# A recurrence and an ELU MLP on one core: the lead-in written in a fixed order, weights fetched in half-step parts on two queues

## The chip, the core and the metric

One core of a Trainium2 chip runs the whole kernel. The metric is device time in microseconds (us) of one launch, the lower the better; the median of three runs of the kernel before is 706.36 us (705.92 to 708.71). Five engines work side by side, each through its own list of instructions in order: PE (matmuls), DVE (vector), ACT (activation functions and copies), POOL (a second, slower elementwise engine) and SP, which here issues transfers and moves nothing else. A transfer (DMA) is issued by an engine's queue and lands later; whoever needs the data waits for it to land.

## What is computed

A gated linear recurrence per head, then an MLP with the ELU function, cut to what matters:

```python
f = 1.0 / (1.0 + np.exp(-f_logit))                 # (B, H, S, D) = (4, 8, 768, 48)
for t in range(S):
    state = f[:, :, t, :, None] * state + np.einsum('bhd,bhe->bhde', k[:, :, t], v[:, :, t])
    y[:, :, t] = np.einsum('bhd,bhde->bhe', q[:, :, t], state)
x = y.transpose(0, 2, 1, 3).reshape(B * S, H * D)  # 3072 x 384
h = x @ w_in                                       # 384 x 2048
g = np.where(h > 0.0, h, np.exp(np.minimum(h, 0.0)) - 1.0)
out = g @ w_out                                    # 2048 x 384
```

The weights arrive as 64-bit floats, 8 bytes an element, 12.6 MB in all.

## The kernel before

**Units.** The 3072 tokens are cut into 12 units of 256 tokens (`U`, `NU`), each of two chunks of 128 (`C`, `NCU`); three units make one batch entry, and the state runs through these three. Heads lie in pairs (`HP` is 4): heads 2p and 2p+1 on the two halves of the partitions, 256 token columns a pair.

**The gates of a unit** (`prepare`, L484). ACT takes Exp of the negated logits (L491), POOL adds 1 (L492), DVE multiplies up along the tokens of one chunk with a scan (L496) and takes the reciprocal (L499). q is multiplied with the reciprocal on DVE (L502), k with the running product on POOL (L503). `fine` (L505) only watches for overflow.

**The recurrence of a unit** (`attention`, L586). For each chunk: `transposed` (k turned on PE, L513, copied by ACT, L515), `scores` (k by q on PE, L524, masked on DVE, L529), `advance` (the state's step: PE L542, DVE L549 and L552), `outputs` (PE L565 and L573, copied to the tile `xt` by ACT, L577). After the second chunk six small transfers inside the core (L584, "the relocations") move the last heads' rows of `xt` to where the MLP wants them.

**The MLP of a unit** has 16 steps, one per 128 columns of the hidden width. `up` (L602): three matmuls into `psH` (two buffers), ACT's Relu and Exp (L611, L612), and DVE's combination of both into `gg` (L614). `down` (L618) follows two steps later (`HLAG`): matmuls of `gg` with `wo` into `psM`.

**The weights** are fetched and turned to 32-bit floats once, while unit 0 runs. `fetch(n)` (L433) brings what step n needs, 128 columns of `w_in` in four transfers and 128 rows of `w_out` in one, 0.786 MB in all, into one of three buffers `raw`. `convert(n)` (L448) does it in integer arithmetic: ACT rounds the low words (L462) and squares the high ones (L463), DVE builds the new bits in two instructions (L464, L468), POOL adds the rounding (L471), and DVE writes `wi` and `wo` (L479), with tiny values set to zero.

**The order** is written in `fast` from L644 on, and a scheduler then places each instruction on its engine: it may pull later work ahead where it thinks that an engine is free. In the first unit's loop (L661 to L682, m = 0) each step converts the weights of one step ahead of its `up`. From unit 1 on nothing is converted.

Of the kernel before, what the change touches and what calls it, by code (L numbers as in the profile page):

```python
# [355 lines left out]
def fast(ctx: ExitStack, tc: tile.TileContext, q, k, v, f_logit, w_in, w_out, out, flag):  # L356
# [23 lines left out]
    HLAG = 2  # L380
    LIMIT = 2.0**60
# [13 lines left out]
    def load(u):  # L395
        b, s0 = u // UPB, (u % UPB) * U
        for n in "fkq":
            for r in range(2):
                nc.sync.dma_start(
                    out=qkf[u % NB][n][HALF[r]],  # L400
                    in_=src[n][b, r::2, :, s0 : s0 + U].rearrange("p d s -> d p s"),
                )
# [3 lines left out]
    for i in range(NB):  # L406
        for n, to in (("f", 50.0), ("k", 0.0), ("q", 0.0)):
            (nc.gpsimd if i else nc.vector).memset(qkf[i][n][:], to)
        if i == 0:
            load(0)  # L410
# [9 lines left out]
    )  # L420
    fine = cst.tile([128, HP, NCU], FP32, name="fine")
# [10 lines left out]

    def fetch(n):  # L433

        c = slice(n * 128, (n + 1) * 128)
        if wide:
            raws[n] = sb.tile([128, 2 * DM], w_in.dtype, tag="raw", name=f"raw{n}", bufs=3)
            di, do = raws[n][:, 0:DM].rearrange("p (k f) -> p k f", k=NKT), raws[n][:, DM:]
        else:
            di, do = wi[:, :, c], wo[:, n, :]  # L440
        main = w_in[0 : NKT * 2 * D, c].rearrange("(k r d) f -> r d k f", r=2, d=D)
        rest = w_in[NKT * 2 * D :, c].rearrange("(k r d) f -> r d k f", r=2, d=PAD)
        for r in range(2):
            nc.sync.dma_start(out=di[64 * r : 64 * r + D], in_=main[r])
            nc.sync.dma_start(out=di[64 * r + D : 64 * r + 64], in_=rest[r])
        nc.sync.dma_start(out=do, in_=w_out[c, :])

    def convert(n):  # L448
# [22 lines left out]
        nc.gpsimd.tensor_tensor(out=bits[:], in0=bits[:], in1=rnd[:], op=ALU.add)  # L471
        val = bits[:].bitcast(FP32)

        for o, a, b in (
            (wi[:, :, n * 128 : (n + 1) * 128], sq[:, 0:DM], val[:, 0:DM]),
            (wo[:, n, :].unsqueeze(1), sq[:, DM:], val[:, DM:]),
        ):
            m = o.shape[1]
            nc.vector.scalar_tensor_tensor(  # L479
                out=o, in0=a.rearrange("p (k f) -> p k f", k=m), scalar=(1.125 * 2.0**-15) ** 2,  # L480
                in1=b.rearrange("p (k f) -> p k f", k=m), op0=ALU.is_ge, op1=ALU.mult,
            )

    def prepare(u):  # L484

        t = qkf[u % NB]
        g = gts[u] = sb.tile([128, HP, U], FP32, tag="g", name=f"g{u}")
        p_ = pts[u] = sb.tile([128, HP, U], FP32, tag="p", name=f"p{u}")
        for h in range(2):
            s = slice(2 * h, 2 * h + 2)  # L490
            nc.scalar.activation(g[:, s], t["f"][:, s], AF.Exp, scale=-1.0)  # L491
            nc.gpsimd.tensor_scalar_add(g[:, s], g[:, s], 1.0)  # L492
            for p in (2 * h, 2 * h + 1):
                for c in range(NCU):
                    a = g[:, p, c * C : (c + 1) * C]
                    nc.vector.tensor_tensor_scan(  # L496
                        out=a, data0=a, data1=a, initial=1.0, op0=ALU.mult, op1=ALU.max
                    )
                    nc.vector.reciprocal(p_[:, p, c * C : (c + 1) * C], a)  # L499
                    if c < NCU - 1:  # L500
                        yield
                nc.vector.tensor_tensor(out=t["q"][:, p], in0=t["q"][:, p], in1=p_[:, p], op=ALU.mult)  # L502
                nc.gpsimd.tensor_tensor(out=t["k"][:, p], in0=t["k"][:, p], in1=g[:, p], op=ALU.mult)  # L503
                yield
        nc.vector.scalar_tensor_tensor(  # L505
            out=fine[:], in0=g[:, :, C - 1 :: C], scalar=LIMIT, in1=fine[:], op0=ALU.is_le, op1=ALU.mult
        )

    def transposed(u, c):

        pt = ps.tile([128, HP, 128], FP32, tag="t", name=f"psT{u}_{c}")
# [43 lines left out]
    def outputs(u, c):  # L555
# [13 lines left out]
        if not first:  # L569
            s = sts.pop((u, c))  # L570
# [158 lines left out]
```

## Time and profile before

| what | value |
|---|---|
| median of 3 runs | 706.36 us |
| the profiled execution: its time / its span | 707.93 us / 706.1 us |
| PE busy in the span | 634.7 us (90%) |
| DVE, ACT, POOL busy | 300.8, 229.3, 105.5 us |
| granted TensorE clock, mean | 0.977 of full speed |
| moved by DMA | 38.04 MB, mean 54 GB/s |

The profiled execution took 707.93 us, 1.6 us over the median of the three runs and 1.8 us over its own span (706.1 us, first to last instruction). A row of a timeline gives the start in us, the duration, the engine, the line of the kernel, the operation, what it writes and reads, how many instructions are merged, and in brackets how long the engine stood idle just before and what released it. PE busy is the share of time in which a matmul was under way, not its speed. PEld is the load of a matmul's stationary side, beside PE.

### The profile page before, as it was taken

Reading aid. Unit: us, or ns where it says so; the run is one execution under the profiler, and the core shown is the slowest. Engines: PE = TensorE matmul, PEld = TensorE weight load, DVE = VectorE, ACT = ScalarE, POOL = GpSimd, SP = SyncE. Lnnn points to the kernel's source line nnn. Section 1 sums busy time; section 2 is a strip of 40 time slices with the busy share of each in tenths; the row PEclk is TensorE's granted clock in tenths of the full one; section 3 lists DMA queues with packets and bytes.
Section 4 is the critical chain, followed back from the end, with each engine's and each line's share of the span. In section 5 each row is a group of like instructions: output and inputs, shape, how many; then the busy total and the mean of one; then the engine's idle time right before and its main releaser. Section 6 shows DMA issues by size and latency. Waiting matters only on the chain.

```text
span 706.1 us, 9060 instructions
## 1 busy us (share of the span) xinstructions
PE 634.7 (90%) x3410; PEld 452.4 (64%) x3410; DVE 300.8 (43%) x599; ACT 229.3 (32%) x509; POOL 105.5 (15%) x102
## 2 busy tenths in 40 slices
PE   0768844569999999999999999999999999999996
PEld 0546522337677777777777777777777777777774
DVE  5889543438852722737124435471226221211110
ACT  2322342343433332333333432423333322333322
POOL 6333223223521101103001101110000000000000
PEclk9999898789999999999999999999999999999999
DMA  9564343432911200200101102011000000000000
GB/s 200 113 124 106 102 123 117 125 77 66 208 24 45 73 23 23 73 23 23 51 23 45 29 27 57 15 45 50 1 24 7 22 1 7 24 1 6 23 0 28
DMA packets 33525, 38.04 MB, mean 54 GB/s; under 512 B 4160, under 2 KB 31424, under 8 KB 33472
## 3 DMA queue, kind: packets, MB, share of 16 engines
q1 hardware_dynamic: 33472, 37.37, 21.2%
q8 instruction: 29, 0.48, 0.3%
q14 instruction: 24, 0.20, 0.1%
HBM read 31.46 MB, written 4.72 MB: 51 GB/s over the span
## 4 chain that ended last, share of the span: by engine, by line
PE 72%; DVE 0%; ACT 0%; issue 0%
PE psH L606 32%; PE psM L624 30%; PE psS L524 3%; PE psY L565 3%; PE psY L573 2%; PE psU L542 1%; PE psT L513 1%; DVE g L496 0%; ACT o L631 0%; DVE gg L614 0%; PE psF L641 0%
## 5 line engine op out<-in xcount | busy, mean ns | idle before, releaser
L606 PE MATMUL psH<-xt,wi 128*128 128x256 f32 x1152 | 295.9, 394 | 23.1 <-DVE wi L479 22.5
L624 PE MATMUL psM<-wo,gg 128*128 128x384 f32 x768 | 283.7, 493 | 13.9 <-DVE gg L614 13.8
L606 PEld LDWEIGHTS psH<-xt,wi 128*128 128x128 f32 x1152 | 216.1, 194 | 89.7 <-DVE wi L479 30.7
L614 DVE SCALAR_TENSOR_TENSOR gg<-e,psH 128x256 f32<-128x256 f32 x192 | 79.6, 414 | 320.6 <-ACT e L612 320.5
L624 PEld LDWEIGHTS psM<-wo,gg 128*128 128x128 f32 x768 | 146.3, 192 | 81.5 <-DVE gg L614 19.9
L611 ACT ACTIVATE e<-psH 128x256 f32<-128x256 f32 x192 | 73.8, 384 | 356.8 <-PE psH L606 353.5
L499 DVE RECIPROCAL p<-g 128x128 f32<-128x128 f32 x96 | 85.2, 920 | 0.3
L612 ACT ACTIVATE e<-e 128x256 f32<-128x256 f32 x192 | 80.0, 417 | 6.0
L503 POOL TENSOR_TENSOR k<-k,g 128x256 f32<-128x256 f32 x48 | 35.0, 746 | 225.4 <-DMA k<-in_k_dram 188.7
L496 DVE TENSOR_TENSOR_SCAN g<-g 128x128 f32<-128x128 f32 x96 | 39.4, 459 | 17.1 <-POOL g L492 17.1
L492 POOL TENSOR_SCALAR g<-g 128x512 f32<-128x512 f32 x24 | 35.4, 1491 | 67.7 <-ACT g L491 67.7
L471 POOL TENSOR_TENSOR bits<-bits,rnd 128x768 int32<-128x768 int32 x16 | 28.9, 1809 | 78.0 <-DVE bits L468 67.0
L524 PEld LDWEIGHTS psS<-q,k 48*128 48x128 f32 x384 | 29.2, 206 | 17.5 <-issue 11.3
L524 PE MATMUL psS<-q,k 48*128 48x128 f32 x384 | 36.5, 313 | 4.0 <-DVE q L502 2.6
L529 DVE TENSOR_TENSOR at<-psS,causal 128x512 f32<-128x512 f32 x48 | 30.9, 681 | 19.8 <-PE psS L524 19.8
L513 PE MATMUL psT<-ident,k 128*128 128x128 f32 x80 | 15.3, 301 | 22.3 <-POOL k L503 22.3
L577 ACT COPY xt<-psY 128x512 f32<-128x512 f32 x24 | 14.0, 585 | 51.1 <-PE psY L573 41.5
L565 PEld LDWEIGHTS psY<-at,v 128*48 128x48 f32 x384 | 21.6, 129 | 13.2 <-issue 6.5
L513 PEld LDWEIGHTS psT<-ident,k 128*128 128x128 f32 x80 | 10.7, 149 | 29.7 <-POOL k L503 24.4
L565 PE MATMUL psY<-at,v 128*48 128x128 f32 x384 | 28.8, 291 | 0.7 <-ACT xt L577 0.7
L515 ACT COPY kn<-psT 128x512 f32<-128x512 f32 x20 | 11.7, 586 | 39.9 <-PE psT L513 39.9
L573 PE MATMUL psY<-q,state 48*48 48x128 f32 x320 | 22.4, 281 | 0.0
(37 smaller groups left out, 188.4 us busy)
## 6 DMA issues: line engine op xcount, KB each, us to landing
raw<-in_moe_w_out_dram SPq DMA_DIRECT2D x16, 384.0 KB, 3.8
v<-in_v_dram SPq DMA_DIRECT2D x12, 384.0 KB, 4.0
raw<-in_moe_w_in_dram SPq DMA_DIRECT2D x32, 144.0 KB, 2.9
f<-in_f_logit_dram SPq DMA_DIRECT2D x24, 192.0 KB, 4.7
k<-in_k_dram SPq DMA_DIRECT2D x24, 192.0 KB, 4.0
q<-in_q_dram SPq DMA_DIRECT2D x24, 192.0 KB, 4.8
out_dram<-o SPq DMA_DIRECT2D x24, 192.0 KB, 1.9
raw<-in_moe_w_in_dram SPq DMA_DIRECT2D x32, 48.0 KB, 2.8
```

The lines of the kernel that those rows point to most:

```text
L492: nc.gpsimd.tensor_scalar_add(g[:, s], g[:, s], 1.0)
L496: nc.vector.tensor_tensor_scan(out=a, data0=a, data1=a, initial=1.0, op0=ALU.mult, op1=ALU.max)
L499: nc.vector.reciprocal(p_[:, p, c * C : (c + 1) * C], a)
L503: nc.gpsimd.tensor_tensor(out=t["k"][:, p], in0=t["k"][:, p], in1=g[:, p], op=ALU.mult)
L524: nc.tensor.matmul(pc[r][:, p], lhsT=t["k"][HALF[r], p, cols], rhs=t["q"][HALF[r], p, cols], start=True, stop=True,)
L565: nc.tensor.matmul(py[HALF[r], p, :], lhsT=vts[u][:, c, h * D : (h + 1) * D], rhs=at[:, r, p], start=(p == 0), stop=first, skip_group_chec ...
L573: nc.tensor.matmul(py[HALF[r], p, :], lhsT=s[HALF[r], p], rhs=t["q"][HALF[r], p, cols], start=False, stop=True, skip_group_check=True,)
L606: nc.tensor.matmul(ph[:], lhsT=wi[:, kt, s * 128 : (s + 1) * 128], rhs=xts[m][:, kt, :], start=(kt == 0), stop=(kt == NKT - 1),)
L611: nc.scalar.activation(e[:], ph[:], AF.Relu, scale=-1.0)
L612: nc.scalar.activation(e[:], e[:], AF.Exp, scale=-1.0)
L614: nc.vector.scalar_tensor_tensor(out=gs[T][:], in0=e[:], scalar=-1.0, in1=ph[:], op0=ALU.add, op1=ALU.max)
L624: nc.tensor.matmul(pms[m][i][:], lhsT=g[:, i * 128 : (i + 1) * 128], rhs=wo[:, s, :], start=(s == 0), stop=(s == NFT - 1),)
```

## The change

In code the change does the following.

- The stretch up to the end of unit 0's MLP stands under `manual_schedule`: its instructions keep the order in which they are written. Work of later units may still be placed between them.
- The two halves of unit 0's f, k and q and of each part of `w_in` go out on two queues, SP's and ACT's (`v`, `w_out` and the later units on SP's alone). Unit 0's logits are the first transfer on both; before, unit 0's `v` (0.39 MB) and a piece of `w_in` (0.15 MB) stood ahead of them on SP. The memsets of unit 0's tiles are shared by DVE and POOL.
- `fetch(n)` brings a part instead of a step: 256 columns of `w_in`, or 256 rows of `w_out`, each 0.786 MB and enough for two steps. Seven buffers `raw` instead of three (`AHEAD`); the order is in `parts`.
- `convert(n)` no longer writes `wi` and `wo`; `place(n)` does, in one instruction of 768 columns instead of two of 384. The rounded words are written back into `raw`, every second 32-bit word, and POOL reads them there. In step s of unit 0 stand `convert(s + 2)`, `place(s + 1)`, `up(s)`, a fetch, `down(s - 2)`.
- The gates: ACT adds the 1 itself (a Copy with a bias). Unit 0 is handled chunk by chunk, two pairs at a time; for all other units one scan runs over 256 columns, made to start again at the second chunk by a tile `restart` and a zero in `f`.
- The recurrence of the next unit stands four steps later in the MLP of a unit (`todo.get(s - 4, ())`); gates are made one unit ahead instead of two.

The core of the diff:

```diff
     def fetch(n):
-        c = slice(n * 128, (n + 1) * 128)
+        j, out_ = parts[n]
+        c = slice(j * 256, (j + 1) * 256)
+        to = wo[:, 2 * j : 2 * j + 2] if out_ else wi[:, :, c]
...
+        for r, e in enumerate((nc.sync, nc.scalar)):
+            e.dma_start(out=to[64 * r : 64 * r + D], in_=main[r])
+            e.dma_start(out=to[64 * r + D : 64 * r + 64], in_=rest[r])
...
-        nc.gpsimd.tensor_tensor(out=bits[:], in0=bits[:], in1=rnd[:], op=ALU.add)
+        nc.gpsimd.tensor_tensor(out=bits[:], in0=bits[:], in1=rnd, op=ALU.add)
+        nc.scalar.activation(sq[:], raw.bitcast(FP32)[:, 1::2], AF.Square)
+        vals[n] = sq, bits
+    def place(n):
...
+        nc.vector.scalar_tensor_tensor(
+            out=to, in0=sq[:].rearrange("p (k f) -> p k f", k=m), scalar=(1.125 * 2.0**-15) ** 2,
+            in1=bits[:].bitcast(FP32).rearrange("p (k f) -> p k f", k=m), op0=ALU.is_ge, op1=ALU.mult,
+        )
...
+            nc.scalar.activation(a, a, AF.Exp, scale=-1.0)
+            nc.scalar.activation(a, a, AF.Copy, bias=1.0)
...
         for s in range(NFT):
             T = m * NFT + s
-            for f in todo.get(s, ()):
+            for f in todo.get(s - 4, ()):
                 f()
-            if m == 0 and ready < NFT:
-                if ready + 1 < NFT:
-                    fetch(ready + 1)
-                convert(ready)
-                ready += 1
+            if m == 0:
+                if s + 2 < NFT:
+                    convert(s + 2)
+                if s + 1 < NFT:
+                    place(s + 1)
             up(T)
+            if m == 0 and s + AHEAD < NFT:
+                fetch(s + AHEAD)
```

DVE in the middle of unit 0's MLP, before: one step's conversion between two `gg` (`gg_4` is step 4's).

```order
L614 SCALAR_TENSOR_TENSOR gg_4_504<-e_4_501,psH_4_497 128x256
L464 TENSOR_SCALAR bits_449<-raw_396 128x768
L468 SCALAR_TENSOR_TENSOR bits_449<-raw_396,bits_449 128x768
L479 SCALAR_TENSOR_TENSOR wi<-sq_448,bits_449 128x3x128
L479 SCALAR_TENSOR_TENSOR wo<-sq_448,bits_449 128x384
L614 SCALAR_TENSOR_TENSOR gg_5_540<-e_5_537,psH_5_533 128x256
```

The same place now, with two masks of unit 1's recurrence in it.

```order
L653 SCALAR_TENSOR_TENSOR gg_3_396<-e_3_393,psH_3_389 128x256
L479 TENSOR_SCALAR bits_410<-raw_241 128x768
L483 SCALAR_TENSOR_TENSOR bits_410<-raw_241,bits_410 128x768
L499 SCALAR_TENSOR_TENSOR wi<-sq_381,bits_382 128x3x256
L653 SCALAR_TENSOR_TENSOR gg_4_424<-e_4_421,psH_4_417 128x256
L568 TENSOR_TENSOR at_0_433<-psS_0_0_434,causal 128x512
L568 TENSOR_TENSOR at_0_433<-psS_0_1_435,causal 128x512
L479 TENSOR_SCALAR bits_447<-raw_322 128x768
```

What DVE writes to `wi` or `wo` (L499) comes from bits that were built one step earlier (bits_382), not from those just built; before it was the same ones (bits_449).

PE at the end of a unit, before: from the last instructions of the next unit's recurrence (`psY`). Unit 4's `psH_0`, which reads the relocated `xt`, follows seven steps later.

```order
L565 MATMUL psY<-at_1_1578,v_1163 48x128 x8
L573 MATMUL psY<-q_72,state_0_1564 48x128 x8
L606 MATMUL psH_9_1716<-xt_1302,wi 128x256 x3
L624 MATMUL psM_0_1547<-wo,gg_7_1662 128x384
L624 MATMUL psM_1_1548<-wo,gg_7_1662 128x384
```

The same place now, in the unit after unit 0.

```order
L604 MATMUL psY<-at_1_908,v_562 48x128 x8
L612 MATMUL psY<-q_75,state_0_894 48x128 x8
L645 MATMUL psH_13_1017<-xt_592,wi 128x256 x3
L663 MATMUL psM_0_808<-wo,gg_11_979 128x384
L663 MATMUL psM_1_809<-wo,gg_11_979 128x384
L645 MATMUL psH_14_1028<-xt_592,wi 128x256 x3
L663 MATMUL psM_0_808<-wo,gg_12_990 128x384
L663 MATMUL psM_1_809<-wo,gg_12_990 128x384
L645 MATMUL psH_15_1039<-xt_592,wi 128x256 x3
L663 MATMUL psM_0_808<-wo,gg_13_1024 128x384
L663 MATMUL psM_1_809<-wo,gg_13_1024 128x384
L645 MATMUL psH_0_1060<-xt_943,wi 128x256 x3
```

Three steps lie between the last `psY` and the `psH_0` that reads the new `xt`.

In the DVE list of unit 0's MLP stand, beside 14 conversions and 15 placings, also the last two pairs of unit 1's gates, four masks and four state instructions of its recurrence, and two pairs of unit 2's gates. Unit 2's recurrence, which stood on PE inside unit 0's MLP before, now stands in unit 1's, but for four score matmuls and two transposes.

## Rows read from the trace of the kernel before

**Rows 1.** Busy time by stretch: PE, PEld, DVE, ACT, POOL, granted clock, DMA share, GB/s
```profile
10.00:27.00 17.00, 7.43 (x46) 4.66 (x46) 14.87 (x28) 4.97 (x8) 7.71 (x7) 1.00 1.10 221
66.70:162.00 95.30, 57.67 (x232) 34.23 (x230) 43.10 (x76) 32.62 (x55) 26.12 (x15) 0.86 0.36 101
162.00:200.00 38.00, 37.48 (x140) 26.94 (x139) 30.68 (x64) 15.44 (x38) 15.10 (x18) 0.96 0.59 128
200.00:300.00 100.00, 100.00 (x575) 72.63 (x574) 45.50 (x98) 34.55 (x81) 14.29 (x14) 1.00 0.17 46
```

**Rows 2.** Timeline, one step of unit 0's MLP
```profile
97.51 0.42 DVE L614 SCALAR_TENSOR_TENSOR gg<-e,psH 128x256 f32<-128x256 f32 x1 [2.05 <-ACT e L612]
97.85 0.55 DVE L464 TENSOR_SCALAR bits<-raw 128x768 int32<-128x768 int32 x1
...
98.43 0.96 DVE L468 SCALAR_TENSOR_TENSOR bits<-raw,bits 128x768 int32<-128x768 int32 x1
...
99.54 1.80 POOL L471 TENSOR_TENSOR bits<-bits,rnd 128x768 int32<-128x768 int32 x1 [5.14 <-DVE bits L468]
...
101.37 0.56 DVE L479 SCALAR_TENSOR_TENSOR wi<-sq,bits 128x384 f32<-128x384 f32 x1 [1.98 <-POOL bits L471]
...
101.98 1.56 PE L606 MATMUL psH<-xt,wi 128*128 128x256 f32 x6 [2.44 <-DVE wi L479]
...
104.45 0.42 DVE L614 SCALAR_TENSOR_TENSOR gg<-e,psH 128x256 f32<-128x256 f32 x1 [2.05 <-ACT e L612]
```

**Rows 3.** Timeline, DVE and POOL at the same moment, three places
```profile
23.29 1.88 POOL L471 TENSOR_TENSOR bits<-bits,rnd 128x768 int32<-128x768 int32 x1 [1.30 <-DVE bits L468]
...
24.61 0.98 DVE L464 TENSOR_SCALAR bits<-raw 128x768 int32<-128x768 int32 x1
...
70.11 1.80 POOL L471 TENSOR_TENSOR bits<-bits,rnd 128x768 int32<-128x768 int32 x1 [4.21 <-DVE bits L468]
...
70.48 1.64 DVE L552 TENSOR_TENSOR state<-state,p 128x192 f32<-128x192 f32 x1
...
159.28 2.95 POOL L492 TENSOR_SCALAR g<-g 128x512 f32<-128x512 f32 x2
...
160.23 0.55 DVE L479 SCALAR_TENSOR_TENSOR wo<-sq,bits 128x384 f32<-128x384 f32 x1
```

**Rows 4.** Timeline, unit 0's gates, and a pair of masks
```profile
7.74 1.28 ACT L491 ACT_TABLE_LOAD   x1 [7.74 <-DMA f<-in_f_logit_dram]
...
9.04 1.15 ACT L491 ACTIVATE g<-f 128x512 f32<-128x512 f32 x2
...
15.45 0.67 DVE L496 TENSOR_TENSOR_SCAN g<-g 128x128 f32<-128x128 f32 x2
...
17.97 0.72 DVE L496 TENSOR_TENSOR_SCAN g<-g 128x128 f32<-128x128 f32 x2
...
27.31 1.28 DVE L529 TENSOR_TENSOR at<-psS,causal 128x512 f32<-128x512 f32 x2
27.54 1.81 POOL L471 TENSOR_TENSOR bits<-bits,rnd 128x768 int32<-128x768 int32 x1 [2.36 <-ACT rnd L462]
```

**Rows 5.** Timeline, the change from unit 0's MLP to unit 1's
```profile
160.36 5.84 PE L606 MATMUL psH<-xt,wi 128*128 128x256 f32 x18 [2.85 <-DVE wi L479]
```

**Rows 6.** Timeline of PE, pieces of a recurrence in the saturated part
```profile
286.18 1.08 PE L573 MATMUL psY<-q,state 48*48 48x128 f32 x16
...
305.39 0.60 PE L513 MATMUL psT<-ident,k 128*128 128x128 f32 x4
308.51 1.16 PE L524 MATMUL psS<-q,k 48*128 48x128 f32 x16
314.97 0.67 PE L542 MATMUL psU<-v,kn 128*64 128x48 f32 x16
```

**Rows 7.** Timeline of SP: one unit's relocations
```profile
287.95 3.68 SPq L584 DMA_DIRECT2D xt<-xt  x6
```

**Rows 8.** Line 584 over the whole trace: from issue to landing
```profile
DMA to landing us min/median/max: 1.7/1.8/4.0
```

More of the change, by code (lines that the diff above doesn't have):

```diff
@@ L393, in fast, with load @@
     vts, gts, pts, ats, kns, xts, sts = {}, {}, {}, {}, {}, {}, {}
-    def load(u):
+    def load(u, other=None):
         b, s0 = u // UPB, (u % UPB) * U
@@ L398, in load @@
             for r in range(2):
-                nc.sync.dma_start(
+                ((other or nc.sync) if r else nc.sync).dma_start(
                     out=qkf[u % NB][n][HALF[r]],
@@ L404, in load, with blank @@
         nc.sync.dma_start(out=vts[u][:], in_=v[b, s0 : s0 + U].rearrange("(c t) n -> t c n", t=C))
[L406 to L410, printed above, removed]
+    def blank(i, *engines):
+        for n, to in zip("fkq", (50.0, 0.0, 0.0)):
+            for j, e in enumerate(engines):
+                w = HP // len(engines)
+                e.memset(qkf[i][n][:, j * w : (j + 1) * w], to)
+    start = ctx.enter_context(ExitStack())
+    start.enter_context(tc.manual_schedule())
+    blank(0, nc.vector, nc.gpsimd)
+    load(0, nc.scalar)
     ident = cst.tile([128, 128], FP32, name="ident")
@@ L420, in fast @@
     )
+    for i in range(1, NB):
+        blank(i, nc.gpsimd)
     fine = cst.tile([128, HP, NCU], FP32, name="fine")
@@ L470, in convert @@
         )
-        nc.gpsimd.tensor_tensor(out=bits[:], in0=bits[:], in1=rnd[:], op=ALU.add)
[L472 to L481, printed above, removed]
-            )
@@ L484, in prepare @@
-    def prepare(u):
[L486 to L507, printed above, removed]
@@ new lines, in decays @@
+    def decays(u, pairs, cols):
+        t = qkf[u % NB]
+        g, p_ = gts[u], pts[u]
+        for p in range(pairs.start, pairs.stop):
+            a = t["f"][:, p, cols]
+            nc.vector.tensor_tensor_scan(
+                out=g[:, p, cols], data0=a, data1=a if cols.stop - cols.start == C else restart[:, p, cols],
+                initial=1.0, op0=ALU.mult, op1=ALU.max,
+            )
+        nc.vector.reciprocal(p_[:, pairs, cols], g[:, pairs, cols])
+        for e, x, y in ((nc.vector, t["q"], p_), (nc.gpsimd, t["k"], g)):
+            e.tensor_tensor(out=x[:, pairs, cols], in0=x[:, pairs, cols], in1=y[:, pairs, cols], op=ALU.mult)
@@ L512, in transposed, with watch @@
+    def watch(u):
+        nc.vector.scalar_tensor_tensor(
+            out=fine[:], in0=gts[u][:, :, C - 1 :: C], scalar=LIMIT, in1=fine[:], op0=ALU.is_le, op1=ALU.mult
+        )
+    def prepare(u):
+        gates(u)
+        yield
+        for p in range(HP):
+            decays(u, slice(p, p + 1), slice(0, U))
+            yield
+        watch(u)
+    def transposed(u, c, bank="t"):
+        pt = ps.tile([128, HP, 128], FP32, tag=bank, name=f"psT{u}_{c}")
         for p in range(HP):
```

106 lines of the change are left out of this document (67 added, 39 removed).

## The prediction

> **What bounds the kernel now.** I read the busy times by stretch first. From 200 us on PE is busy in all of every stretch at full clock; from 66.7 to 162 us, while unit 0's MLP runs, it is busy for 57.7 of 95.3 us, at a mean granted clock of 0.86 [rows 1]. So the end is PE's list, and what can be won lies before 162 us. Next, the timeline of one step of that MLP: from one `gg` to the next are 6.94 us, and each instruction in between waits for the one before it: DVE builds the bits (0.55 and 0.96), POOL adds (1.80), DVE writes `wi` (0.56), PE runs `up` (1.56), ACT its two functions, DVE the next `gg` (0.42) [rows 2]. No engine is full; the chain through four of them is the bound, because DVE stands in `wi` for POOL and converts nothing meanwhile. Twelve of the 16 steps run so, the first four being ahead.
>
> **How I count.** t1 is the moment at which PE begins unit 1's first `up`. Before, 18 matmuls (three steps' `up`) start at 160.36 and take 5.84; the second third starts at 162.3 [rows 5]. From there to the end of the span are 706.1 - 162.3 = 543.8 us, nearly all of it full PE. The change moves one thing into this stretch: unit 2's recurrence, which on PE costs one group of transposes, two of scores, one of `psU` and four of `psY`: 0.60 + 2 x 1.16 + 0.67 + 4 x 1.08 = 7.9 us [rows 6], less 0.6 for what is still pulled ahead. So the new span is t1 + 543.8 + 7.3 = t1 + 551.1, and t1 is what has to be worked out.
>
> **The lead-in up to step 0's converting.** The logits land at 7.74 now [rows 4], behind 0.54 MB that no longer stand ahead of them, 2.4 us at 221 GB/s [rows 1]: 5.3 to 7.7 us. A table load of 1.28 and two ACT instructions of 0.58 follow [rows 4]; POOL's addition leaves this path, its work is ACT's now. First scan at 7.8 to 10.2; I take 8.2, since the queue ahead is empty. DVE then has: four lots of gates of 256 columns, 2.52 us each (from 15.45 to 17.97 [rows 4]), 10.1; two pairs of masks, 1.28 each [rows 4]; three state instructions, an estimate of 0.35 each from the masks' 0.64 for 512 columns; two conversions of 0.58 + 0.96 and one placing. The placing is one instruction of 768 columns with two SBUF inputs, as is the second bits instruction: 0.96 [rows 2]. Then two pairs of unit 1's gates, 5.0. In order: 8.2 + 10.1 + 1.7 = 20.0; conversion 0 to 21.5; masks to 22.8, under POOL's addition (21.6 to 23.4); conversion 1 to 24.9; placing 0 to 25.8; POOL's addition 1 to 27.6 (why DVE waits here comes below); a pair, two state instructions, a pair: 33.4. `gg` of step 0 needs `up`, and that the relocations: chunk 1's masks at 22.8, `psY`, a copy, 3.68 of issue and 1.8 of landing [rows 7, 8] make 33; but they also stand on SP behind five weight parts, and 7.9 MB at 221 GB/s take 36 us. `gg_0` at 36 to 43, I take 40. DVE with POOL behind it would be there at 37.7, so 2.3 us are lost.
>
> **A step of unit 0's MLP after the change.** Written so, DVE has 0.58 (to the start of the next, 97.85 to 98.43) + 0.96 + 0.96 + 0.42 = 2.92 us a step [rows 2], PE at most 2.7 (543.8 us less nine recurrences of 7.9, over the 178 steps in it), POOL 1.80. If the three ran freely, DVE's 2.92 would be the step. They don't. Where POOL's addition ran from 23.29 to 25.17, DVE's first bits instruction took 0.98 instead of 0.55 and ended 0.42 after POOL; where it ran from 70.11 to 71.91, a state product over 192 columns took 1.64 and ended 0.21 after POOL [rows 3]. So an addition of this kind holds up DVE's work on two SBUF tensors, and its first bits instruction, to its end. Masks and `gg`, with one input from PSUM, and reciprocals, with one input, I count as free: the two masks of 27.31 took 0.64 each though such an addition began at 27.54 [rows 4]. Then per step the bits, the placing and POOL's addition stand one behind the other, 0.58 + 0.96 + 0.96 + 1.80 = **4.30 us**, with `gg` and masks (0.42 + 1.28) under the addition. A third place speaks against a rule for all POOL work: beside POOL's tensor_scalar of 159.28 a placing of 384 columns took its usual 0.55 [rows 3].
>
> The Trainium skill, page "SBUF — State Buffer", section "Who interferes with whom", has a rule that speaks against this change: DVE with two SBUF inputs, or in a two-port mode, and a POOL instruction that reads SBUF exclude one another, and the second waits for all of the first. By that rule the step is 4.30 and the span 660, as by the first two places; by the third the step would be near 2.92 and the span 646. The trace agrees at two places of three.
>
> ACT has two instructions of 768 and two of 256 columns a step, at its 0.58 for 512 [rows 4] some 2.3 to 2.7 us, and every second step two transfers to issue; it fits under 4.30. Issuing on ACT costs what is queued behind it: `Relu` and `Exp` of the same step, whose `gg` has over a microsecond to spare. A part of 0.786 MB takes 3.6 us at 221 GB/s [rows 1], under 4.30, and seven are ahead, so weights are hidden as long as they come faster than 183 GB/s. SP's relocations of unit 1 are issued four steps before t1 and hidden too.
>
> **The sum.** From 33.4: 2.3 lost at `gg_0`; 14 steps with a conversion, 60.2; the last placing and `gg_14`, 1.4; two pairs of unit 1's gates and two of unit 2's in DVE's list, 4 x 2.52 = 10.1; two state products that can't hide, 0.7. That is 74.7, t1 = 108.1, span 659.2. In unit 1 DVE has the gates of units 2 to 4 to make up; before, PE idled 0.5 us of 162 to 200 at a clock of 0.96 [rows 1], which is in the 551.1; I add 1. **660 us of span**, 46 less. The profiled execution was 707.93 us for 706.1 of span, the median 706.36 stands just over the span, so against the median I forecast 660. Bounds of the terms: first scan +2.0; `gg_0` -2 to +3; state products -0.7 to +1; a step 4.1 (waits overlapping) to 4.5 (0.2 of handovers), -3 to +3; unit 1's make-up -1 to +4.
>
> **Rivals.**
> - *POOL doesn't hold DVE up.* The third place of rows 3 speaks for it, the first two against. Step 2.92, masks 2.6 and all state work 1.4 no longer hidden: start 31.1, wait for `gg_0` 6.4, then 40.9 + 1.4 + 10.1 + 4.0; t1 = 93.9, span 645 to 646. Chance 0.13.
> - *The clock.* From 66.7 to 162 us the mean clock was 0.86, which is the lower of the two levels (1.2 against 2.4 GHz) for 28% of the time, with PE busy 60% [rows 1]. At the lower level PE needs up to 5.3 us a step and passes DVE. Against it: PE will be busy some 60 to 70%. Over all 16 steps it costs 16 x 1.0 = 16 and unit 1's recurrence 8: 676 to 684. Chance 0.10.
> - *Given back at the borders of units.* The last `psY` is three steps ahead of the next `psH_0` instead of seven, 8 us; copy, issue and landing need 6.2 (287.26 to 291.63 and 1.8 [rows 6 to 8]). A landing of 4.0, the longest [rows 8], is 0.4 over. At 1 to 2 us each, ten borders cost 10 to 20: 670 to 680. It decides from 8 us on. Chance 0.07.
> - *Weights too late*, the two queues not doing what they are for: below 183 GB/s each us of a later part is a us of the step; at 150, 5.2 a step: 673. Chance 0.04.
> - *Slower than before: POOL's new addition.* Its second input now lies in every second word of `raw`; no row shows POOL reading so. Place: all 14 additions of unit 0's MLP, each in the serial 4.30. A us more costs 14 us; it decides from 1.80 + 46 / 14 = 5.1 us an addition. At three times the price, 5.4, the span is 710. For it: nothing but that it is unseen; the nearest row, the dense one, is 1.80. Chance 0.04; twice the price (685) is in the range's end.
>
> The Trainium skill, page "GPSIMD Engine Reference", section "7. Performance pitfalls for Q7 kernels", has the step between elements cost half as much again above 8 bytes; here it is 8. By it the price stays; one step over it would be 2.7 us an addition and 672 in the sum. No run here shows it.
>
> **How the numbers follow.** The forecast, 660 (648 to 672), has 0.62. The range must take in the first rival below and most of the clock and the borders above: **645 to 684**. Two runs of this kernel can be told apart from about 0.5%, 3.5 us. Faster by more than that: all cases but the last and a sliver of the others, 0.94; within it 0.02; slower 0.04.
>
> **What would show it.** Right: `gg` to `gg` in unit 0's MLP 4.1 to 4.6 us in steps without gates; DVE's bits instruction shown as 1.5 to 2 us where POOL's addition runs; unit 1's first `up` at 105 to 112; PE full from then on. Steps near 3 us mean the first rival, matmul groups of six near 2.9 us the clock, PE waiting at each `psH_0` the borders, POOL's addition over 2.2 us the last. The whole is wrong if PE is not full behind t1, since all of the gain is t1.

## The result and the profile after

The changed kernel takes 671.43 us (median of four runs, 670.13 to 673.12) against 706.4 for the kernel before (median of four): a ratio of 0.950 with a 95% interval of 0.947 to 0.953. I had forecast 660 with a range of 645 to 684. The mechanism is the forecast one; the time is 11 us above the forecast, and nearly all of that lies ahead of t1. The profiled execution took 673.12 us, for a span of 671.4 us.

The changed kernel by stretch, with the columns of [rows 1]. The first row is the stretch in which unit 0's MLP ran before; the last one begins with PE's first matmul of unit 1 (t1).

```profile
66.70:162.00 95.30, 84.56 (x489) 58.96 (x488) 84.13 (x118) 52.21 (x103) 42.87 (x50) 0.97 0.54 116
162.00:200.00 38.00, 38.00 (x190) 27.64 (x186) 8.55 (x19) 14.08 (x34) 0.00 (x0) 1.00 0.15 43
200.00:300.00 100.00, 100.00 (x572) 72.82 (x572) 47.65 (x80) 34.61 (x83) 7.90 (x17) 1.00 0.16 43
117.60:162.00 44.40, 41.89 (x237) 29.47 (x235) 39.08 (x61) 21.37 (x48) 15.36 (x32) 1.00 0.28 63
```

PE was busy for 57.7 of the 95.3 us before and is for 84.6 now, at a clock of 0.97 instead of 0.86. From 162 us on it is full, as before. From t1 to 162 it stands idle for 2.5 us, all of it in unit 1, waiting for `gg`.

Now one step of unit 0's MLP, which answers to [rows 2]. Timeline of the changed kernel, with the rows of other engines left out.

```profile
63.65 0.95 DVE L499 SCALAR_TENSOR_TENSOR wo<-sq,bits 128x768 f32<-128x768 f32 x1
63.95 2.36 POOL L486 TENSOR_TENSOR bits<-bits,raw 128x768 int32<-128x768 int32 x1 [1.71 <-DVE bits L483]
64.51 0.41 DVE L653 SCALAR_TENSOR_TENSOR gg<-e,psH 128x256 f32<-128x256 f32 x1
...
64.84 1.88 DVE L479 TENSOR_SCALAR bits<-raw 128x768 int32<-128x768 int32 x1
...
66.76 0.96 DVE L483 SCALAR_TENSOR_TENSOR bits<-raw,bits 128x768 int32<-128x768 int32 x1
...
67.63 0.95 DVE L499 SCALAR_TENSOR_TENSOR wi<-sq,bits 128x768 f32<-128x768 f32 x1
...
68.50 0.41 DVE L653 SCALAR_TENSOR_TENSOR gg<-e,psH 128x256 f32<-128x256 f32 x1
```

From `gg` to `gg` are 3.99 us, where 6.94 were. DVE has no gap, yet it does not work all the time: its first bits instruction, 0.55 us alone, is shown as 1.88 and ends 0.41 us after POOL's addition (66.72 against 66.31). POOL's 2.36 in turn holds a wait: it is shown from 63.95, and DVE's placing ends at 64.60; from there to 66.31 are 1.7. `gg`, which reads PSUM, takes its usual 0.41 meanwhile. What is no longer in the chain is PE and ACT.

Where the time above the forecast came from stands in the lead-in. DVE, ACT and SP in the changed kernel, up to `gg_0`:

```profile
25.51 0.32 ACTq L459 DMA_DIRECT2D raw<-in_moe_w_in_dram  x1
...
32.54 0.32 ACTq L460 DMA_DIRECT2D raw<-in_moe_w_in_dram  x1
32.96 0.63 ACT L515 ACTIVATE f<-f 128x512 f32<-128x512 f32 x1 [7.29 <-DMA raw<-in_moe_w_in_dram]
...
34.77 0.69 DVE L526 TENSOR_TENSOR_SCAN g<-f,restart 128x256 f32<-128x256 f32 x1 [6.83 <-ACT f L515]
...
35.34 0.57 ACT L616 COPY xt<-psY 128x512 f32<-128x512 f32 x1
...
35.93 6.40 SPq L623 DMA_DIRECT2D xt<-xt  x6
...
37.28 1.62 DVE L532 TENSOR_TENSOR q<-q,p 128x256 f32<-128x256 f32 x1
...
42.54 0.55 DVE L479 TENSOR_SCALAR bits<-raw 128x768 int32<-128x768 int32 x1
...
48.10 0.42 DVE L653 SCALAR_TENSOR_TENSOR gg<-e,psH 128x256 f32<-128x256 f32 x1 [3.15 <-ACT e L651]
```

ACT issues one transfer of part 5 at 25.51 and the next only at 32.54. In between it computes nothing: unit 1's gates (L515) and the copy of unit 0's last `xt` (L616) are queued behind that issue. DVE waits 6.83 us for the gates, and the relocations cannot be issued before the copy. What the issue stood for can be read from the landing times in the trace: eight transfers were under way, on both queues together. SP's issue at 31.82 went out 0.02 us after one of them had landed (31.80), and ACT's at 32.54 0.02 us after the next (32.52, a part of `w_out` that had been issued at 20.15 and took 12.4 us to land). In none of the 14 traces kept here are more than eight transfers under way, whatever the queue; eight are reached 10 to 48 times in each. Whether the chip or the program's own semaphores set this number, no run here tells.

### The profile page after: what moved, and what is told of

Its sections match the earlier page's. It is cut to its first block, busy times and chain, and to the rows that moved or that the text cites. A ratio compares the mean times of both kernels' runs of the same rounds, so it can differ in the third digit from the quotient of the medians.

```text
span 671.4 us, 8938 instructions
## 1 busy us (share of the span) xinstructions
PE 617.4 (92%) x3410; PEld 445.6 (66%) x3410; DVE 301.3 (45%) x491; ACT 240.2 (36%) x533; POOL 92.1 (14%) x126
## 3 DMA queue, kind: packets, MB, share of 16 engines
q1 hardware_dynamic: 27344, 33.63, 21.0%
## 4 chain that ended last, share of the span: by engine, by line
PE 79%; DMA 8%; DVE 7%; POOL 2%; ACT 2%; issue 1%; SPq 0%; POOLq 0%; DVEq 0%; ACTq 0%
PE psH L645 35%; PE psM L663 33%; DMA f<-in_f_logit_dram 4%; DMA raw<-in_moe_w_in_dram 3%; PE psY L604 3%; PE psS L563 3%; PE psY L612 3%; DVE p L530 2%; DVE g L526 2%; PE psU L581 1%; POOL bits L486 1%; DMA xt<-xt 1%; PE psT L552 1%; DVE bits L483 1%; DVE q L532 0%
## 5 line engine op out<-in xcount | busy, mean ns | idle before, releaser
L645 PE MATMUL psH<-xt,wi 128*128 128x256 f32 x1152 | 290.4, 389 | 21.1 <-DMA xt<-xt 16.2
L530 DVE RECIPROCAL p<-g 128x256 f32<-128x256 f32 x48 | 83.0, 1740 | 0.6
L532 POOL TENSOR_TENSOR k<-k,g 128x256 f32<-128x256 f32 x48 | 37.1, 795 | 260.9 <-DMA k<-in_k_dram 160.1
L486 POOL TENSOR_TENSOR bits<-bits,raw 128x768 int32<-128x768 int32 x16 | 37.1, 2317 | 34.3 <-DVE bits L483 12.1
L563 PEld LDWEIGHTS psS<-q,k 48*128 48x128 f32 x384 | 25.2, 198 | 14.3 <-issue 13.8
L526 DVE TENSOR_TENSOR_SCAN g<-f,restart 128x256 f32<-128x256 f32 x44 | 30.9, 749 | 8.3 <-ACT f L515 6.8
L616 ACT COPY xt<-psY 128x512 f32<-128x512 f32 x24 | 14.0, 584 | 55.1 <-PE psY L612 41.5
L563 PE MATMUL psS<-q,k 48*128 48x128 f32 x384 | 30.3, 298 | 0.6 <-DVE q L532 0.3
L515 ACT ACTIVATE f<-f 128x512 f32<-128x512 f32 x24 | 14.6, 624 | 25.2 <-DMA f<-in_f_logit_dram 16.2
L532 DVE TENSOR_TENSOR q<-q,p 128x256 f32<-128x256 f32 x48 | 21.9, 457 | 0.3
```

The source lines that it names most:

```text
L486: nc.gpsimd.tensor_tensor(out=bits[:], in0=bits[:], in1=rnd, op=ALU.add)
L526: nc.vector.tensor_tensor_scan(out=g[:, p, cols], data0=a, data1=a if cols.stop - cols.start == C else restart[:, p, cols], initial=1.0, o ...
L530: nc.vector.reciprocal(p_[:, pairs, cols], g[:, pairs, cols])
L532: e.tensor_tensor(out=x[:, pairs, cols], in0=x[:, pairs, cols], in1=y[:, pairs, cols], op=ALU.mult)
L563: nc.tensor.matmul(pc[r][:, p], lhsT=t["k"][HALF[r], p, cols], rhs=t["q"][HALF[r], p, cols], start=True, stop=True,)
L645: nc.tensor.matmul(ph[:], lhsT=wi[:, kt, s * 128 : (s + 1) * 128], rhs=xts[m][:, kt, :], start=(kt == 0), stop=(kt == NKT - 1),)
```

## The experiments

Each kernel was timed against the kernel before. The first `gg` and t1 are read from the profiles; behind t1 is the span less t1.

| kernel | median us | ratio, 95% interval | gg_0 | t1 | behind t1 |
|---|---|---|---|---|---|
| the kernel before | 706.4 | | 51.2 | 161.8 | 544.3 |
| the change | 671.4 | 0.947 to 0.953 | 48.1 | 117.6 | 553.8 |
| 1 parts 5, 6 late | 666.8 | 0.941 to 0.946 | 41.8 | 108.8 | 555.7 |
| 2 weights on SP | 665.0 | 0.938 to 0.942 | 48.7 | 113.0 | 552.2 |
| 3 no addition | 660.3 | 0.931 to 0.936 | 45.5 | 107.6 | 552.4 |
| 4 order kept through unit 1 | 676.0 | 0.953 to 0.958 | 46.4 | 107.4 | 566.2 |
| 5 = 1 and 2 | 658.9 | 0.929 to 0.934 | 38.1 | 102.3 | 552.9 |
| 6 = 5, a pair of gates earlier | 655.8 | 0.925 to 0.930 | 38.8 | 101.5 | 552.1 |
| 7 scheduler's order | 673.4 | 0.949 to 0.954 | 64.6 | 117.4 | 554.9 |
| 8 unit 0 whole | 671.9 | 0.948 to 0.953 | 47.0 | 116.1 | 553.8 |
| 9 no lag | 682.1 | 0.961 to 0.967 | 50.5 | 134.0 | 548.2 |
| 10 before, fixed order | 700.9 | 0.988 to 0.993 | 55.1 | 147.3 | 554.2 |
| 11 = 10 with the lag | 695.5 | 0.981 to 0.986 | 53.5 | 141.7 | 551.2 |
| 12 dense rounding | 670.7 | 0.945 to 0.950 | 47.7 | 116.9 | 553.8 |

The expectations of experiments 1 to 4 count from a t1 of 120.2 for the change. That is unit 1's second `up`; its first begins at 117.6, so what they say of t1 is to be read as a difference to 120.2.

### The lead-in: who stands in front of an issue

My theory after the result: ACT's own issues hold up its computing. The rival: the transfers are the limit, and any wait that is removed comes back as a wait for weights.

Experiment 1:

```diff
     scores(0, 1)
-    fetch(5)
-    fetch(6)
...
     watch(0)
     next(steps)
+    fetch(5)
+    fetch(6)
```

> Parts 5 and 6 of the weights are fetched after unit 1's first two pairs of gates and after unit 0's relocations, instead of ahead of them. In the changed kernel ACT stood from 25.83 to 32.54 us in front of a transfer that it was to issue, and DVE waited 6.8 us for unit 1's gates. Theory (ACT's own issues hold up its computing): ACT makes the gates at about 26, DVE's wait of 6.8 is gone, conversion 2 starts at 35 to 36 instead of 42.5, gg_0 at 39 to 42 instead of 48.1, t1 at 112 to 114 instead of 120.2, span 663 to 665. Rival (the transfers themselves are the limit: 221 GB/s flat up to 40 us): the wait returns as a wait of ACT's rounding or DVE's bits for parts 5 to 7, t1 at 118 to 121, span 669 to 672.

ACT, SP and DVE of this kernel:

```profile
24.96 0.62 ACT L515 ACTIVATE f<-f 128x512 f32<-128x512 f32 x1
...
28.77 7.70 SPq L623 DMA_DIRECT2D xt<-xt  x6
...
30.60 0.32 ACTq L459 DMA_DIRECT2D raw<-in_moe_w_in_dram  x1
...
35.38 0.55 DVE L479 TENSOR_SCALAR bits<-raw 128x768 int32<-128x768 int32 x1
...
37.30 0.32 ACTq L460 DMA_DIRECT2D raw<-in_moe_w_in_dram  x1
...
41.81 0.42 DVE L653 SCALAR_TENSOR_TENSOR gg<-e,psH 128x256 f32<-128x256 f32 x1 [4.02 <-ACT e L651]
```

ACT still stands from 30.92 to 37.30 in front of an issue, but nothing that DVE needs is behind it now. The gates are made at 24.96, conversion 2 starts at 35.38 instead of 42.54, t1 is 8.8 us earlier. The rival, that the wait returns as a wait for weights, is out. The edit moves two things, though: ACT's issues behind the gates, and SP's issues of the same parts behind the relocations. Experiment 2 moves the first alone. The span fell by 6.9 (the medians by 4.6) and not by 8.8: PE waits in unit 1 for `gg` for 3.1 us.

Experiment 2:

```diff
-        for r, e in enumerate((nc.sync, nc.scalar)):
+        for r, e in enumerate((nc.sync, nc.sync)):
             e.dma_start(out=to[64 * r : 64 * r + D], in_=main[r])
```

> All weight transfers go out on SP; ACT issues only its three of unit 0. Theory (ACT's own issues hold it up): DVE's wait of 6.8 us before unit 1's gates is gone and conversion 2 starts at 35 to 37; but unit 0's relocations still stand behind parts 5 and 6 on SP, so gg_0 comes only 1 to 4 us sooner (44 to 47); t1 116 to 119, span 667 to 670. Rival (two queues are needed to bring the weights in time): waits of 1 us and more a step for raw words in unit 0's MLP, span above 675.

SP and DVE of this kernel; the stretch from 27 to 40 us of it, with the columns of [rows 1]; and the same stretch of the changed kernel:

```profile
33.63 7.34 SPq L623 DMA_DIRECT2D xt<-xt  x6
...
48.70 0.42 DVE L653 SCALAR_TENSOR_TENSOR gg<-e,psH 128x256 f32<-128x256 f32 x1 [12.72 <-ACT e L651]
```

```profile
27.00:40.00 13.00, 0.00 (x0) 0.00 (x0) 8.77 (x12) 2.63 (x4) 5.66 (x4) 0.66 1.07 216
```

```profile
27.00:40.00 13.00, 1.09 (x20) 0.81 (x16) 6.07 (x8) 6.01 (x9) 3.31 (x6) 0.63 1.06 221
```

DVE is done with conversion 2 9.0 us earlier (placing 1 starts at 35.02 instead of 44.00, not shown), and then waits 12.72 us, because the copy of `xt` was ready at 26.4 and the relocations stand on SP behind parts 5 and 6 until 33.63. So freeing ACT alone does not bring `gg_0` forward, which I had not expected: the relocations then wait for weights on SP, and from their first issue to `up(0)` are 11.3 us (33.63 to 44.90, the latter not shown). t1 is 4.6 us earlier all the same: unit 2's gates come behind the conversions now and not between them, and no step waits for their logits. One queue brings 216 GB/s where two bring 221: the second queue carries no weights faster, and taking it away makes the kernel 6.4 us faster. The Trainium skill, page "DMA: Bandwidth & Descriptors", section "Issuing engines are not separate DMA queues", says the same, that issuing on several engines saves only the time of issuing; the trace agrees with these two rows.

Experiment 5 joins both edits.

> The two edits of the first two experiments together: all weight transfers on SP, and parts 5 and 6 fetched behind unit 0's relocations. Alone they brought PE's first matmul of unit 1 (t1) from 117.6 us to 108.8 and to 113.0. Theory (each removes another wait: ACT standing in front of an issue, and the relocations standing behind weights): they add up, gg_0 at 40 to 42, steps of 3.99 from the third on, t1 at 104 to 106, span 656 to 659. Rival (once these are gone the transfers are the limit, weights come too late): waits of 1 us and more a step for raw words, t1 at 108 or later, span 662 or more.

They add up: `gg_0` at 38.1, t1 at 102.3, both some 2 us better than expected, and 658.9. ACT has no wait for raw words in its steps, which was the rival's mark.

Experiment 6 puts one more `next(steps)` ahead of the loop in this version, so that a pair of gates stands where DVE had waited.

> As the run before, and one pair of unit 1's gates (2.9 us of DVE) is moved from step 0 of unit 0's MLP to ahead of it, where DVE waits 4.0 us for gg_0 in the version with parts 5 and 6 late on two queues. Theory (that wait is for the relocations, not for DVE): 2.5 to 3.0 us less than the run before, span 653 to 656. Rival (gg_0 moves back by as much as DVE is delayed): the same as the run before within 1.

The median is 3.1 us lower, and each of its four times lies under each of experiment 5's; but the intervals of the ratios touch, and in the profiles t1 moved by under 1 us. The 4.0 us of wait on which I had counted were those of experiment 1; in experiment 5 only 1.2 were left (38.07, not shown). This is the fastest kernel of the study, 2.4% under the changed one by the two ratios.

Experiment 8 takes the other part of the lead-in back: `gates(0)` in whole units and all four pairs ahead of chunk 0's recurrence.

> Unit 0's gates in whole units instead of chunk by chunk: four lots of one pair by 256 columns (2.9 us each, as much DVE work), all four ahead of chunk 0's recurrence instead of two; the logits go through POOL's restart column as for the other units. Theory (the 6.8 us for which ACT stands in front of its issue cover the recurrence's delay of some 5 us): 671 to 673, t1 117 to 120. Rival (chunk by chunk is on the path to gg_0): 3 to 6 us more, 674 to 677.

671.85, the same as the change. Beside ACT's 6.8 us chunk by chunk is worth nothing; whether it is once they are gone (experiment 5) was not tried.

### The step: DVE and POOL

Experiment 3 removes one line, POOL's addition of the rounded words.

```diff
-        nc.gpsimd.tensor_tensor(out=bits[:], in0=bits[:], in1=rnd, op=ALU.add)
```

> Leaves out POOL's addition of the rounded low words, so the weights are cut off instead of rounded; nothing else is changed. Theory (the step of 3.99 us is DVE's work on two SBUF tensors and POOL's addition one behind the other): steps without gates fall to 2.7 to 3.0 us, what DVE itself needs, DVE's first bits instruction is 0.55 us everywhere instead of 1.88; 14 steps save 1.1 to 1.2 each, masks and state work that were hidden come back with 3 to 4: t1 105 to 110, span 656 to 661. Rival (DVE is not held up, the step is some other wait): steps stay within 0.3 of 3.99 and the span within 3 of 671.4.

A step of this kernel on DVE:

```profile
59.54 0.41 DVE L652 SCALAR_TENSOR_TENSOR gg<-e,psH 128x256 f32<-128x256 f32 x1
59.87 0.55 DVE L479 TENSOR_SCALAR bits<-raw 128x768 int32<-128x768 int32 x1
...
60.46 0.96 DVE L483 SCALAR_TENSOR_TENSOR bits<-raw,bits 128x768 int32<-128x768 int32 x1
...
61.33 0.95 DVE L498 SCALAR_TENSOR_TENSOR wi<-sq,bits 128x768 f32<-128x768 f32 x1
...
62.20 0.41 DVE L652 SCALAR_TENSOR_TENSOR gg<-e,psH 128x256 f32<-128x256 f32 x1
```

2.66 us instead of 3.99, and the first bits instruction takes 0.55 in 15 of 16 places (the other, 1.08 at 94.7, runs beside POOL's product of k; not shown). t1 is 10.0 us earlier and the time 660.3, both as expected. In the changed kernel nothing on DVE waits for this addition's result in the same step, and still it costs 1.33 us of each plain step. A step with two masks gains nothing: 4.05 us here (62.20 to 66.25, not shown) against 4.00, since the masks had stood beside the addition. This is the exclusion that the prediction took from [rows 3]. The Trainium skill's page "SBUF — State Buffer", section "Who interferes with whom", has it as a lock under which the second waits for all of the first; with 1.88 against 0.55 the trace agrees. The third place of [rows 3], POOL's tensor_scalar, is no longer in the changed kernel, and no run settles it.

Experiment 9 puts the placing behind its own conversion (`place(s + 2)` in step s).

> The changed kernel with the placing of a part right behind its own conversion, in the same step, instead of one step later; order, parts, queues and gates stay. DVE then waits in the placing for POOL's addition of the same part. Theory (a step is DVE's two bits, POOL's addition and the placing one behind the other; the lag only puts gg and masks beside POOL's addition): steps of 4.6 to 4.8 us instead of 3.99 and masks no longer hidden, 14 x 0.7 + 2.6 = 12 us more, span 680 to 686. Rival (the lag carries most of the gain over the kernel before): steps near 6.9, span 700 and more.

DVE and POOL of this kernel:

```profile
68.10 1.85 POOL L486 TENSOR_TENSOR bits<-bits,raw 128x768 int32<-128x768 int32 x1 [3.09 <-DVE bits L483]
...
69.99 0.96 DVE L499 SCALAR_TENSOR_TENSOR wi<-sq,bits 128x768 f32<-128x768 f32 x1 [2.11 <-POOL bits L486]
70.87 0.41 DVE L653 SCALAR_TENSOR_TENSOR gg<-e,psH 128x256 f32<-128x256 f32 x1
```

Steps of 4.9 us (the `gg` before is at 65.92, not shown) and 682: the lag is worth 0.9 us a plain step and some 10 us of the time, and not the whole gain. t1 is 16.4 us later than with the lag, but 5.6 of them come back behind t1: there PE no longer waits, and more of unit 2's recurrence is done by then.

Experiment 12 gives the rounded words a dense tile again.

> The changed kernel with the rounded low words in a tile of their own, read densely by POOL, instead of in every second word of the raw part (and two output tiles instead of three, to make room for it). Theory (the step between elements costs POOL next to nothing): additions that start with DVE idle take 1.80 instead of 1.85 to 1.98, steps 3.9 to 4.0, span 669 to 672. Rival (the step costs a tenth or more of each addition, 0.2 us in 14 serial steps): 3 us less or more, 666 to 668.

An addition of this kernel that starts beside no work of DVE on two SBUF tensors and, in the second fence, the same one of the changed kernel:

```profile
36.56 1.81 POOL L486 TENSOR_TENSOR bits<-bits,rnd 128x768 int32<-128x768 int32 x1 [0.92 <-ACT rnd L478]
```

```profile
36.77 1.85 POOL L486 TENSOR_TENSOR bits<-bits,raw 128x768 int32<-128x768 int32 x1 [0.92 <-ACT raw L478]
```

1.81 against 1.85: every second word costs POOL next to nothing, and 670.7 is the same time as the change's. The Trainium skill's rule on the step (page "GPSIMD Engine Reference", section "7. Performance pitfalls for Q7 kernels"), of which the prediction said that no run here showed it, agrees at its 8 bytes.

### The order

Experiment 7 leaves out the fixed order.

```diff
-    start.enter_context(tc.manual_schedule())
```

> The changed kernel without the fixed order: the scheduler places the lead-in and unit 0's MLP itself; all else stays (parts, two queues, in-place rounding, lag of the placing, gates). It puts all of unit 0's gates ahead of the conversions, a weight part ahead of the logits on ACT, and converts up to seven parts ahead of gg_0. Theory (the gain is in the serial step of DVE and POOL, 4.0 instead of 6.94, and that comes from placing a step later, not from the order): span 666 to 678. Rival (the fixed order carries the gain): 690 and more.

673.4, with t1 at 117.4. The scheduler converts so far ahead that `gg_0` comes at 64.6 instead of 48.1, and the steps behind it are then shorter; t1, at 117.4 against 117.6, is the same. With all the rest of the change in place the fixed order is worth 0 to 2 us.

Experiments 10 and 11 go the other way: the kernel before, with the fixed order alone, and with the order and the lag (its placing still two instructions).

```diff
+    start = ctx.enter_context(ExitStack())
+    start.enter_context(tc.manual_schedule())
     AHEAD = 3
...
+        if m == 0:
+            start.close()
```

> The kernel before with one part of the change alone: the lead-in and unit 0's MLP keep the order in which they are written. As written, step s converts what step s + 2 needs; the scheduler had let it slip until PE's matmuls waited for the weights of the same step, which put PE and ACT into the chain of 6.94 us. Theory (a fixed order takes PE and ACT out of the chain): steps of 4.8 to 5.0 us (0.58 + 0.88 for the bits, 1.80 and two handovers of 0.1 for POOL, twice 0.48 for the placings, 0.34 for gg), and against that a lead-in in which nothing overlaps that was not written so: t1 at 130 to 140 instead of 162, span 674 to 688. Rival (the order brings nothing without seven buffers and two queues): steps of 6 and more, span 700 and more.

DVE of this kernel behind `gg_0` and in a plain step, and one row of ACT:

```profile
55.05 0.41 DVE L614 SCALAR_TENSOR_TENSOR gg<-e,psH 128x256 f32<-128x256 f32 x1
...
59.38 4.13 DVE L496 TENSOR_TENSOR_SCAN g<-g 128x128 f32<-128x128 f32 x8
...
63.12 0.93 ACT L462 ACTIVATE rnd<-raw 128x768 int32<-128x768 uint32 x1 [7.32 <-DMA raw<-in_moe_w_out_dram]
...
68.30 0.41 DVE L614 SCALAR_TENSOR_TENSOR gg<-e,psH 128x256 f32<-128x256 f32 x1
...
73.11 0.41 DVE L614 SCALAR_TENSOR_TENSOR gg<-e,psH 128x256 f32<-128x256 f32 x1
```

The plain step is 4.81 us, as expected, but the time is 700.9 where I had expected 674 to 688. I had summed plain steps. Here the gates of unit 2 stand in every second step, eight scans of a later unit stand behind `gg_0`, and from there to `gg_1` are 13.25 us. The rival has a part in that one gap: ACT waits until 63.12 for a weight part, so without the scans DVE would have waited too. Ahead of t1 DVE makes the gates of four units (32 reciprocals of 0.95 us), where it had made those of three (24), and t1 is at 147.3. That is 14.5 us earlier than in the kernel before, of which 9.9 are given back behind t1, because most of unit 2's recurrence now stands there.

> As the run before, and the placing (still two instructions) is put one step behind its conversion. Theory: steps of 4.0 to 4.2, gg and masks beside POOL's addition; 10 to 13 us less than the run before. Rival (with three buffers the weights come too late for 4.1 a step): steps of 4.6 and more, under 6 us less.

One step of it, on DVE and POOL:

```profile
129.74 0.55 DVE L486 SCALAR_TENSOR_TENSOR wi<-sq,bits 128x384 f32<-128x384 f32 x1
129.97 1.99 POOL L471 TENSOR_TENSOR bits<-bits,rnd 128x768 int32<-128x768 int32 x1 [2.35 <-DVE bits L468]
130.21 2.17 DVE L486 SCALAR_TENSOR_TENSOR wo<-sq,bits 128x384 f32<-128x384 f32 x1
...
132.30 0.41 DVE L621 SCALAR_TENSOR_TENSOR gg<-e,psH 128x256 f32<-128x256 f32 x1
```

5.4 us less than experiment 10, not 10 to 13, and neither expectation names the reason: in the plain steps weights are not late. POOL's addition slips in between the two placings, the second of them is shown as 2.17 us instead of 0.55, and `gg` waits behind it. The step is 4.35 (from 127.95, not shown). So the one placing of 768 columns is a part of the change with a worth of its own: it leaves only `gg` and masks, which read PSUM, for the time of POOL's addition.

Experiment 4 asks what unit 2's gates cost ahead of t1; it keeps the order to the end of unit 1 (`if m == 1: start.close()`).

> The fixed order is kept to the end of unit 1's MLP instead of unit 0's, so unit 2's gates are no longer placed inside unit 0's MLP. Theory (unit 2's gates in ACT's, POOL's and DVE's lists ahead of t1 cost about 9 us: 2.9 ACT waiting for logits that have not landed, 1.3 DVE waiting for POOL's restart column, 5 of DVE work): t1 at 110 to 113 instead of 120.2; in unit 1 DVE then has 2.9 of gates a step in four steps beside gg, more than PE's 2.585, which gives back 3 to 6: span 664 to 668. Rival (all is given back in unit 1, because PE waits there for DVE): span 670 to 673.

t1 came 10.2 us earlier, at 107.4, where 7 to 10 were expected, and the time is 676.0, worse than both theories said. PE of this kernel in unit 1, and what DVE did:

```profile
118.53 3.33 DVE L530 RECIPROCAL p<-g 128x256 f32<-128x256 f32 x2
...
119.46 0.33 PE L552 MATMUL psT<-ident,k 128*128 128x128 f32 x1 [1.34 <-POOL k L532]
...
124.55 0.47 PE L552 MATMUL psT<-ident,k 128*128 128x128 f32 x1 [4.77 <-POOL k L532]
...
157.19 2.93 PE L645 MATMUL psH<-xt,wi 128*128 128x256 f32 x6 [3.43 <-DVE gg L653]
```

The transposes of unit 2 stand in PE's list ahead of `up`, and wait for gates that DVE had not made yet; the scheduler had also put unit 3's gates between them (two reciprocals in one row). PE waits 9.5 us behind t1 where it waited 2.5, and its groups of six take 2.77 (at 124.82, not shown) and 2.93 after the two longest waits instead of 1.46. 10.2 us of t1 were given back as 12.4 behind it. Gates ahead of t1 cost less than PE's wait for them behind it.

## The prediction, step by step

| term | forecast | measured |
|---|---|---|
| first scan | 8.2 | 7.93 |
| a lot of gates of 256 columns | 2.52 | 2.9 |
| step 0's converting | 33.4 | 42.54 |
| gg_0 | 40 | 48.10 |
| a plain step | 4.30 | 3.99 |
| gg_0 to t1 | 68.1 | 69.5 |
| t1 | 108.1 | 117.6 |
| behind t1 | 552.1 | 553.8 |
| span | 660 | 671.4 |

**Right: the bound and the count by t1.** All of the gain is t1. PE is full from 162 us on, and the 552.1 us behind t1, with unit 2's recurrence in them, were missed by 1.7. The reserve for unit 1's gates, 1 us and the 0.5 that the 551.1 held, was 1.0 too small: PE waits 2.5 us there. Another 0.5 is a reading: in the kernel before unit 1's first `up` begins at 161.8 and not at 162.3.

**Right: POOL's addition and DVE's work exclude one another.** Experiment 3 shows it from one side (2.66 us without the addition), the 1.88 of the bits instruction from the other. The first rival, with its 2.92 us a step, is out. The step was 0.31 too long in the sum, because I added 0.96 for instructions whose starts follow one another after 0.87, and took POOL's addition to end before the first bits instruction begins, while it ends 0.4 before that one does.

**Wrong: the price of issuing on ACT.** The step that failed is the sentence that issuing on ACT costs what is queued behind it, `Relu` and `Exp` of the same step, with over a microsecond to spare. It was looked at for the steps alone and priced by the issue's own time. In the lead-in the gates of unit 1 and the copy of `xt` are queued behind it, and an issue can stand for longer than it takes: 6.7 us, with eight transfers under way. DVE's wait of 6.83 is most of the 9.1 us by which conversion 2 is late; 1.2 more are q times p held by POOL's addition (1.62 us at 37.28), and 0.8 the two lots of gates. Experiment 2 took ACT's weight issues away alone: conversion 2 came 9.0 us earlier, t1 4.6.

**Wrong: the relocations in the lead-in.** `gg_0` came 8.1 us later than the 40 of the sum, past its bound of +3, and stayed late in experiment 2 (48.7). The prediction gave the relocations 3.68 of issue and 1.8 of landing, 5.5 us, from rows of the saturated part. From their first issue to `up(0)` are 8.4 us in the changed kernel (35.93 to 44.30), 9.2 in experiment 1, where they start 7.2 us sooner, 11.3 in experiment 2 and 6.4 in experiment 5 (27.84 to 34.26, not shown): six small transfers wait for a place among the eight, with weight parts under way. Experiment 1 changed both, ACT's wait and the place of the relocations, and took 8.8 us off t1; experiment 5, with no weights on ACT either, 15.3.

So t1, at 117.6, lies outside the 105 to 112 that the prediction had given as its mark. The time lies inside the 648 to 672 of the main case by 0.6 us. That is luck: steps that were too long in the sum made up for a part of what the lead-in cost.

**Mis-sized: the way from gg_0 to t1.** The 13 steps behind `gg_0` were 0.31 shorter (-4.0). Against that, four lots of gates were 0.4 longer (+1.5), and two waits were in no term (+4.2). Together that is +1.7, against 1.4 measured. Timeline of ACT, SP and DVE in the changed kernel at `gg_8`:

```profile
78.74 1.00 SPq L401 DMA_DIRECT2D f<-in_f_logit_dram  x2
...
86.74 0.63 ACT L515 ACTIVATE f<-f 128x512 f32<-128x512 f32 x1 [4.67 <-DMA f<-in_f_logit_dram]
87.27 0.40 ACT L651 ACTIVATE e<-e 128x256 f32<-128x256 f32 x1
...
87.70 0.42 DVE L653 SCALAR_TENSOR_TENSOR gg<-e,psH 128x256 f32<-128x256 f32 x1 [2.88 <-ACT e L651]
...
89.92 0.69 DVE L526 TENSOR_TENSOR_SCAN g<-f,restart 128x256 f32<-128x256 f32 x1 [1.33 <-POOL f L519]
```

The scheduler had put unit 2's gates between ACT's two functions of step 8. Their logits had not landed, so `Exp` of the step waited behind them, and DVE 2.88 us for it; 1.33 more for POOL's restart column. I had counted these gates on DVE and not looked at ACT's list.

**The other rivals.** The clock stayed at its upper level from 60 us on but for short stretches (0.97 from 66.7 to 162 us); at the lower of the two levels, 1.2 GHz, it was after PE's idle 16 us ahead of `up(0)` (0.50 from 44.30 to 47.30, not shown), and again after a wait of 3.2 us ahead of 92.92 (0.50 from 92.90 to 95.70, not shown). Nothing is given back at the borders of units: PE is busy for 100.00 of 100 us. Weights were in time: in the steps ACT waits for a part once, for 0.55 us (at 66.83, not shown). POOL's addition costs no more with every second word (experiment 12), so the slower case had no ground.

**What carries the 35 us** was taken apart only in part. Undone alone, the lag costs some 10 us, and the fixed order, the chunk-wise lead-in and the in-place rounding cost 0 to 2; the weights' second queue is a loss of some 6 (experiment 2). Added alone to the kernel before, the order brings 6 us, and order and lag 12. The rest, some 23 us, goes with what was not tried alone: parts for two steps in seven buffers, the placing in one instruction, and gates one unit ahead instead of two. The traces point to the last of these. Summed up, DVE spends 52.5 us on gates (scans, reciprocals and products with q) ahead of t1 in experiment 11 and 34.5 in the changed kernel: 18.0 of the 24.1 us between their t1. That is an argument from the traces; no run has this alone.

## What to carry to other kernels

An engine that computes should issue a transfer only where nothing urgent is queued behind the issue, since an issue can stand until earlier transfers have landed. To price a step that two engines share, look first for instructions that are shown longer than alone, and put between them what reads PSUM. Before moving work out of the stretch that you shorten, look at what waits for it in the next one.

## What was not expected of the hardware

Issues stand in their queue when several transfers are under way: six relocations took 3.68 us to issue in the saturated part [rows 7], and 6.40, 7.34 and 7.70 in the lead-ins shown here. In the changed kernel eight transfers are issued by 4 us, and the ninth goes out at 5.58, after the first had landed (ACT starts on its data at 5.31). With the count over all traces above, that reads like a limit of eight that the two queues share; no run was made to test it.

Of DVE's instructions beside POOL's addition, the scan over two SBUF tensors is held too (2.00 us instead of 0.69, at 53.95 of the changed kernel, not shown). A product of two SBUF tensors was 1.29 instead of 0.35 (at 77.21), while the sum of a PSUM and an SBUF tensor just ahead of it took its 0.35 under the same addition (at 76.82).
